# Transposing u by the DMA crossbar instead of on TensorE, with the loads of each stretch moved forward

## The chip, the cores and the metric

The kernel runs on one core of one Trainium2 chip. The metric is device time of one execution in microseconds (us). Times of one kernel mostly agree within 0.3%. Engines are named as in the profile: PE is TensorE's matmul stream, PEld its weight loads, DVE is VectorE, ACT is ScalarE, POOL is GpSimd, SP is SyncE, and SPq is SP's own queue, which issues DMAs one after the other. L followed by a number is a line of that kernel's file, so line numbers differ from kernel to kernel. A DMA's landing is the moment when its data are reported as in place; the granted clock is the share of PE's full clock that it was given.

## The reference, cut to what matters

Eight batches of 576 rows and 512 columns go through a retention layer (attention with a decay mask), then a mixer: a low-rank product over the sequence gives h, u = x + h, and a two-layer network runs on u.

```python
def _moe_ref(x, U, V, w_ch1, w_ch2):      # x: retention output, (8, 576, 512)
    xt = x.transpose(0, 2, 1)
    h = xt @ U @ V                         # rank 32, over the sequence
    u = x + h.transpose(0, 2, 1)
    ch = np.maximum(u @ w_ch1, 0.0) @ w_ch2   # 512 -> 2048 -> 512
    return (u + ch).astype(np.float32)
```

The first layer contracts over the 512 columns of u. TensorE contracts over partitions, so u, which is produced with rows on partitions, has to be transposed first. That transpose is what the change is about.

## The kernel before

Two batches form a pair of 1152 rows, which is nine chunks of 128 rows. An even batch takes four chunks into its network, an odd batch five. The work is merged into stretches: in the stretch of batch b the "main" list is the network of batch b (first layer Y1, then second layer Y2), and two "fill" lists are spread between its items: the attention and mixer of batch b+1, and "aux", the loads and preparations (cast, scaling, transposes of q and k by the crossbar) for later batches. A lead of 0.93 means that a fill's last item lies near 93% of the main list's matmul cost.

```python
LEAD = 0.93
def merge(main, *fills):
    total = sum(c for c, _ in main)
    ...
        queues.append([((k + 0.5) / n * LEAD * total, fn) for k, fn in enumerate(fill)])
    ...
# the mixer of one batch: MA (low rank), then per group of two chunks MH (h and u) and MT (transpose u)
outs = [(0, 1), (2, 3)] if par == 0 else [(4, 5), (6, 7), (8,)]
...
    def MT(grp):
        n, l0 = len(grp), grp[0] - base
        pu = ps_sc.tile([P, 2, NCC, P], BF16, tag="psc", name="pu")     # PSUM
        for s in range(n):
            for cc in range(NCC):                                       # NCC = 4
                nc.tensor.transpose(pu[:, s, cc, :],
                    st["u", par][:, l0 + s, cc * P:(cc + 1) * P], ident)
        nc.scalar.activation(out=st["uT", par][...], in_=pu[:, 0:n, :, :], func=AF.Copy)
...
    # first layer, for each of 16 blocks f of 128 columns
    for t0, n in segs:                     # [(0, 512)] even, [(0, 320), (320, 320)] odd
        for cc in range(NCC):
            nc.tensor.matmul(ps[:, 0:n], w1_sb[:, cc, f * P:(f + 1) * P],
                             st["uT", par][:, cc, t0:t0 + n], ...)
...
# aux, for chunk g: load(g) issues three DMAs on SP; prep(g - 2) casts, scales and issues
# one crossbar transpose of q and k, 128x1024, also on SP
for b in range(2, B):
    merge(y1_items(par) + y2_items(pr, par), fill, aux)
```

## Time and profile before

| | before |
|---|---|
| time, median | 366.6 us |
| PE busy from 98.5 to 289 us | 190.5 of 190.5 us |
| PE transposes of u | 144, in 20 groups |
| ACT evictions of uT | 20 |
| crossbar transposes on SP | 27, all of q and k, 128x1024 |

The table of busy time by stretch, kernel before. The columns are the window, its length, then busy time and instruction count of PE, PEld, DVE, ACT and POOL, then the granted clock of PE, the mean DMA share and GB/s.

```profile
98.50:134.50 36.00, 36.00 (x235) 17.27 (x233) 14.21 (x19) 6.35 (x10) 8.82 (x12) 1.00 0.84 189
134.50:169.40 34.90, 34.90 (x273) 17.26 (x271) 14.82 (x19) 16.69 (x28) 6.42 (x8) 1.00 0.60 134
169.40:211.40 42.00, 42.00 (x363) 25.20 (x361) 16.97 (x22) 20.74 (x44) 8.13 (x10) 1.00 0.76 157
```

PE is busy for the whole of each window. What leaves PE here should shorten the kernel; what leaves ACT should not.

The chain of waits in order of time, kernel before, at the end of batch 2's stretch (start, us, what):

```profile
161.63 0.43 PE ph L370 x2
162.06 0.45 PE pu L383 x8
162.50 1.73 PE ps_y L436 x8
164.23 0.22 PE ph L370
164.45 0.45 PE pu L383 x8
164.89 1.73 PE ps_y L436 x8
166.62 0.22 PE pu L383 x4
166.84 2.59 PE ps_y L436 x12
169.43 2.17 PE ps_y L415 x16
```

Eight transposes of u (pu) take 0.45 us, 56 ns each; eight 512-column matmuls take 1.73 us, 216 ns each. The last line is the first layer of batch 3, which starts with no gap.

The view of one tile, qkT, kernel before: the crossbar transposes that already exist (minimum, median and maximum of the time that SP's queue takes to issue one, in ns), and the time from issue to landing of all of them.

```profile
L201 SPq DMA_TRANSPOSE qkT<-qk x27: 1232/1253/4160, 65.2 to 284.3; - x27
DMA to landing us min/median/max: 3.0/3.2/6.5
```

Both maxima belong to the first transpose, at 65.2 us.

### The profile page before, as it was taken

What the parts mean: (1) busy time and instruction counts of PE and PEld (TensorE: products, weight loads), DVE (VectorE), ACT (ScalarE), POOL (GpSimd) and SP (SyncE); (2) the same over time, 40 slices, a digit from 0 to 9 for tenths busy, and PEclk for the clock granted to TensorE, in tenths of its full rate; (3) what the DMA queues carried; (4) which work ended last, traced back from release to release, by engine and by line L of the source; (5) the groups of instructions that cost most, each with busy time, mean ns of one, the idle gap of its engine ahead of it and who ended that gap; (6) DMA issues with size and microseconds to landing.
All of it is one profiled execution on the core that took longest, in us unless ns stands there. A gap on an engine that the chain in (4) does not pass through costs nothing.

```text
span 366.2 us, 6281 instructions
## 1 busy us (share of the span) xinstructions
PE 327.5 (89%) x2600; PEld 181.7 (50%) x2600; DVE 130.0 (36%) x180; ACT 162.3 (44%) x300; POOL 78.5 (21%) x114
## 2 busy tenths in 40 slices
PE   1466758899999999999999999999999999999990
PEld 0343334357644445545764545457754454567540
DVE  2354223442335414453343434443344144400110
ACT  4341446578710226425771266137732463258200
POOL 7166172220022240024102220122013100010010
PEclk9999978999999999999999999999999999999996
DMA  9999999997686982597567786786564300110010
GB/s 162 220 181 198 217 216 199 213 202 132 121 171 182 203 202 62 111 208 192 119 120 166 178 145 116 172 160 130 116 145 94 108 0 3 57 59 0 30 77 37
DMA packets 149820, 49.65 MB, mean 136 GB/s; under 512 B 143264, under 2 KB 147488, under 8 KB 149792
## 3 DMA queue, kind: packets, MB, share of 16 engines
q1 hardware_dynamic: 141024, 35.40, 51.9%
q0 software_dynamic: 8768, 13.86, 15.3%
q8 instruction: 20, 0.33, 0.4%
q14 instruction: 8, 0.07, 0.1%
HBM read 37.14 MB, written 9.44 MB: 127 GB/s over the span
## 4 chain that ended last, share of the span: by engine, by line
PE 50%; issue 28%; SPq 8%; POOL 5%; DMA 3%; ACT 2%; DVE 2%; POOLq 0%
PE ps_y L436 21%; PE ps_y L415 20%; SPq L174 8%; POOL vt L193 3%; PE psc L228 2%; PE po L267 2%; POOL out_dram L445 2%; DMA stage_t<-in_v_dram 1%; PE pu L383 1%; DMA stage_t<-in_q_dram 1%; DVE ret L238 1%; PE pss L293 1%; PE ph L370 1%; ACT qkT L214 1%; ACT y L420 1%
## 5 line engine op out<-in xcount | busy, mean ns | idle before, releaser
L415 PE MATMUL ps_y<-uT,w_sb 128*128 128x320 bf16 (+1 forms) x768 | 138.1, 330 | 3.5 <-ACT y L420 2.4
L436 PE MATMUL ps_y<-w_sb,y 128*128 128x512 bf16 x576 | 132.0, 379 | 0.0
L420 ACT ACTIVATE y<-ps_y 128x320 bf16<-128x320 f32 (+1 forms) x192 | 93.4, 490 | 53.6 <-PE ps_y L415 43.1
L415 PEld LDWEIGHTS <-w_sb 128*128 128x128 bf16 x768 | 72.4, 99 | 47.1 <-issue 5.9
L436 PEld LDWEIGHTS <-y 128*128 128x128 bf16 x576 | 54.0, 98 | 61.9 <-issue 2.5
L445 POOL DMA_DIRECT2D out_dram<-o_sb x36 | 20.3, 564 | 231.3 <-DVE o_sb L442 160.6
L238 DVE TENSOR_TENSOR ret<-psc,tri 128x1024 bf16<-128x1024 f32 x32 | 39.2, 1225 | 71.7 <-PE psc L228 71.7
L442 DVE TENSOR_TENSOR o_sb<-ps_y,u 128x512 f32<-128x512 f32 x36 | 24.8, 690 | 67.2 <-PE ps_y L436 67.1
L193 POOL TENSOR_TENSOR vt<-stage_t,vscale 128x512 bf16<-128x512 f32 x36 | 37.7, 1056 | 47.2 <-DMA stage_t<-in_v_dram 23.8
L387 ACT ACTIVATE uT<-pu 128x1024 bf16<-128x1024 bf16 (+1 forms) x20 | 18.8, 939 | 46.2 <-PE pu L383 46.2
L278 DVE TENSOR_TENSOR xt<-po,qscale 128x512 bf16<-128x512 f32 x36 | 24.9, 691 | 40.2 <-PE po L267 36.4
L373 DVE TENSOR_TENSOR u<-ph,xt 128x1024 bf16<-128x1024 f32 (+1 forms) x20 | 22.4, 1118 | 32.0 <-PE ph L370 32.0
L186 ACT ACTIVATE qk<-stage_t 128x512 bf16<-128x512 f32 x36 | 22.3, 623 | 10.4 <-DMA stage_t<-in_q_dram 10.4
L301 ACT ACTIVATE s_sb<-pss 128x512 bf16<-128x512 f32 x32 | 19.1, 596 | 17.0 <-PE pss L293 16.0
L351 ACT ACTIVATE a_sb<-pa 128x512 bf16<-128x512 f32 x8 | 4.8, 597 | 44.2 <-PE pa L346 44.2
L210 PE MATMUL pst<-ident,qk 128*128 128x128 bf16 x72 | 8.4, 288 | 15.1 <-ACT qk L186 15.1
L184 DVE CAST qk<-stage_t 128x512 bf16<-128x512 f32 x36 | 16.0, 444 | 10.3 <-DMA stage_t<-in_k_dram 10.3
L267 PE MATMUL po<-vt,ret 128*128 128x64 bf16 x288 | 15.6, 201 | 3.6 <-DVE ret L238 2.8
L267 PEld LDWEIGHTS <-ret 128*128 128x128 bf16 x288 | 13.7, 103 | 10.0 <-DVE ret L238 4.0
L228 PE MATMUL psc<-qkT 64*128 64x128 bf16 x288 | 15.6, 233 | 2.7 <-DVE ret L238 1.3
L228 PEld LDWEIGHTS <-qkT 64*128 64x128 bf16 x288 | 8.9, 100 | 15.5 <-issue 10.9
L210 PEld LDWEIGHTS <-qk 128*128 128x128 bf16 x72 | 6.8, 132 | 17.7 <-ACT qk L186 16.5
(47 smaller groups left out, 125.0 us busy)
## 6 DMA issues: line engine op xcount, KB each, us to landing
out_dram<-o_sb POOLq DMA_DIRECT2D x36, 256.0 KB, 2.8
stage_t<-in_k_dram SPq DMA_DIRECT2D x32, 256.0 KB, 4.1
stage_t<-in_q_dram SPq DMA_DIRECT2D x32, 256.0 KB, 4.7
stage_t<-in_v_dram SPq DMA_DIRECT2D x32, 256.0 KB, 5.1
w_sb<-in_moe_w_ch_dram POOLq DMA_DIRECT2D x16, 128.0 KB, 6.8
w_sb<-in_moe_w_ch_dram POOLq DMA_DIRECT2D x8, 256.0 KB, 9.4
stage_t<-in_k_dram SPq DMA_DIRECT2D x8, 128.0 KB, 3.4
stage_t<-in_q_dram SPq DMA_DIRECT2D x8, 128.0 KB, 3.6
```

What stands on the lines that cost most here:

```text
L174: nc.sync.dma_start(out=c["f"][rows, j, :, :], in_=dram[b, :, t0:t0 + n, :].rearrange("h s d -> s h d"),)
L193: nc.gpsimd.tensor_tensor(out=c["v"], in0=c["f"][:, 2, :, :], in1=vscale[:, i, :, None].to_broadcast([P, H, D]), op=ALU.mult,)
L228: nc.tensor.matmul(psc[:, hl, hp, :], qkT[r, NHP + hp, :], qkT[r, hp, :], start=True, stop=True,)
L238: nc.vector.tensor_tensor(out=ret.rearrange("p (hp hl) i -> p hl hp i", hl=2), in0=c["psc"], in1=m[:, None, None, :].to_broadcast([P, 2, N ...
L267: nc.tensor.matmul(c["po"][:, hl, hp * D:(hp + 1) * D], c["ret"][:, h, :], c["v"][:, h, :], start=(first and hp == 0), stop=True, skip_gro ...
L278: nc.vector.tensor_tensor(out=xt[:, i, :].rearrange("p (hp hl d) -> p hl hp d", hl=2, d=D), in0=c["po"][:, :, 0:NHP * D].rearrange("p hl ( ...
L373: nc.vector.tensor_tensor(out=st["u", par][:, i0 - base:i0 - base + n, :], in0=ph[:, 0:n, :], in1=st["x", pr][:, i0:i0 + n, :], op=ALU.add,)
L415: nc.tensor.matmul(ps[:, 0:n], w1_sb[:, cc, f * P:(f + 1) * P], st["uT", par][:, cc, t0:t0 + n], start=(cc == 0), stop=(cc == NCC - 1),)
L420: nc.scalar.activation(out=st["y1", par][:, f, t0:t0 + n], in_=ps[:, 0:n], func=AF.Relu)
L436: nc.tensor.matmul(ps, st["y1", par][:, f, c * P:(c + 1) * P], w2_sb[:, f, :], start=(f == 0), stop=(f == NF - 1),)
L442: nc.vector.tensor_tensor(out=o_sb, in0=ps, in1=st["u", par][:, c, :], op=ALU.add)
L445: nc.gpsimd.dma_start(out=out_flat[r0:r0 + P, :], in_=o_sb)
```

## The change

From batch 2 on, u is no longer transposed on PE and evicted by ACT. Each chunk, 128x512, goes through the DMA crossbar from SBUF to SBUF, issued on SP right after u of its group exists. The aux list now ends near 0.7 of the stretch, so that the loads pause when these transposes need SP and the DMA engines. The other fill ends near 0.9.

```diff
-LEAD = 0.93
-def merge(main, *fills):
+def merge(main, *fills, leads=(0.9, 0.7)):
...
-        queues.append([((k + 0.5) / n * LEAD * total, fn) for k, fn in enumerate(fill)])
+        queues.append([((k + 0.5) / n * lead * total, fn) for k, fn in enumerate(fill)])
...
         def MT(grp):
             n, l0 = len(grp), grp[0] - base
+            if pr > 0:
+                for s in range(n):
+                    nc.sync.dma_start_transpose(
+                        out=st["uT", par][:, :, (l0 + s) * P:(l0 + s + 1) * P],
+                        in_=st["u", par][:, l0 + s, :],
+                    )
+                return
...
                 if m < len(outs):
                     MH(outs[m])
-                if m > 0:
+                if pr > 0:
+                    if m < len(outs):
+                        MT(outs[m])
+                elif m > 0:
                     MT(outs[m - 1])
```

More of the change, by code (lines that the diff above doesn't have):

```diff
@@ L13 @@
 ALU = mybir.AluOpType
-LEAD = 0.93
-def merge(main, *fills):
+def merge(main, *fills, leads=(0.9, 0.7)):
     total = sum(c for c, _ in main)
     queues = []
-    for fill in fills:
+    for fill, lead in zip(fills, leads):
         n = len(fill)
-        queues.append([((k + 0.5) / n * LEAD * total, fn) for k, fn in enumerate(fill)])
+        queues.append([((k + 0.5) / n * lead * total, fn) for k, fn in enumerate(fill)])
     done = 0.0
```

## The prediction

> **What bounds the kernel now.** From about 85 us on, TensorE. The table of busy time by stretch gives PE 36.00 of 36.00 us in 98.5-134.5, 34.90 of 34.90 in 134.5-169.4, 42.00 of 42.00 in 169.4-211.4, and so on to about 349 us, at granted clock 1.00; DVE and ACT are about 40-50% busy. Before 85 us the start-up bounds: DMA share 9 tenths, and a chain of waits over load issues and ACT/DVE hand-offs. The change hardly touches that part.
>
> **Removed.** Batches 2 to 7 have 27 row chunks of u, four 128x128 transposes each: 108 of the 144 PE transposes. In the chain, eight take 0.45 us of PE (56 ns each), so 108 x 56 ns = 6.0 us, all where PE is never idle: all on the critical path. Also 15 ACT evictions of uT (1.02 us, 0.60 for the half tile), about 14 us off the path: worth nearly nothing.
>
> **Added.** 27 crossbar transposes of 128x512 on the SP queue. The 27 existing ones of 128x1024 take SP 1.23 us to issue and land after 3.1-3.2 us in the steady part (6.5 at worst, while loads saturated the queues at 65 us). I estimate half the issue, 0.65 us, plus the same tail of 1.9 us: 2.5 us alone, 3.2 us for two in a row. The Trainium skill ("DMA: Bandwidth & Descriptors", Issuing engines are not separate DMA queues) says all DMAs share the same 16 engines and interleave; the 6.5 us agrees. Hence the change's second half: loads end at about 0.66 of a stretch's matmul work and the u transposes come after.
>
> **Is the new latency hidden?** In the changed instruction order, a batch's last h matmul is followed by 28 second-layer matmuls (28 x 216 ns = 6.05 us) where an even batch comes next, 24 (5.2 us) where an odd one does, 44 at the first boundary. Even: DVE add 1.23, hand-offs 0.2, transposes 3.2: about 4.7 us. Odd: one chunk, 0.69 + 0.2 + 2.5 = 3.4 us. Both fit with over 1 us to spare: no PE stall, or a few tenths at one or two boundaries.
>
> **Moved.** A chunk's load comes every 5.9 us rather than 7.8. Queue 1 took 51.9% of the span for 36 chunks and 27 transposes, about 5 us each, so the DMA share rises to 0.85-0.95 in the load part. Casts come two loads (11 us) after issue, against landings of 4-7 us, so ACT and DVE should not stall. In the stretch after start-up (48-85 us) casts come earlier, but after the loads land; its remaining PE transposes sit closer (12 in a row): perhaps 0.4 us lost.
>
> **Prediction.** 366.6 - 6.0 + 0.2 to 0.4 = 360.8 us (-1.6%), range 359.3 to 363.3. Faster by over 2%: 0.10; within 2%: 0.86; slower: 0.04.
>
> **What would show it.** pu transposes fall from 144 to 36, uT evictions from 20 to 5; each stretch from 98 us on shortens by 0.9 (even batch's transposes gone) or 1.1 us (odd); u transposes land within 2.2-3.5 us; first-layer matmuls wait under 1 us in total for uT.
>
> **What would make it wrong.** The 128x512 transposes landing in 4 us or more (or traffic still in the queues): a stall at each of six boundaries, where 1 us each eats the gain. SP stuck on a late cast ahead of them. ACT starved of casts by compressed loads, with PE stalls in first-layer phases. Or the first stretch shifting by over 1 us.

## The result, and the profile after

The changed kernel takes 363.57 us (four runs, 363.13 to 363.83) against 366.6 us: ratio 0.991, 95% interval 0.989 to 0.993. A ratio here and below is the mean time of one kernel's fast runs over that of the other's fast runs of the same rounds, so it is not quite the ratio of the medians. Executions over 1.5% slower than the fastest of the same kernel are left out of the means. The gain is 3.0 us where 5.8 were forecast, and the time lies 0.3 us outside the range. The single profiled executions differ by 4.2 us (spans 366.2 and 362.0), but there the first layer of batch 0 happens to start 1.1 us earlier; I therefore compare stretches, not spans.

The same windows, kernel after:

```profile
98.50:134.50 36.00, 35.59 (x209) 16.41 (x213) 14.30 (x19) 3.68 (x7) 8.41 (x13) 1.00 0.92 190
134.50:169.40 34.90, 33.76 (x255) 16.77 (x259) 14.81 (x19) 14.57 (x27) 7.42 (x10) 1.00 0.77 163
169.40:211.40 42.00, 41.75 (x343) 24.03 (x345) 17.73 (x22) 18.85 (x43) 7.75 (x11) 1.00 0.88 172
```

In the middle window PE now shows 1.1 us without work: 0.7 us are one wait, explained below, and 0.3 us are two gaps of 0.15 to 0.16 us with 7 matmuls shown in place of 8, which I take to be missing records. The DMA share has risen by 0.08 to 0.17.

SP's timeline, kernel after, around the end of batch 2's stretch (start, us, what, count):

```profile
155.99 2.44 SPq L199 DMA_TRANSPOSE qkT<-qk  x1
158.58 6.64 SPq L380 DMA_TRANSPOSE uT<-u  x5
165.32 0.74 SPq L172 DMA_DIRECT2D stage_t<-in_k_dram  x1
```

PE's timeline, the same time:

```profile
161.01 0.38 PE L368 MATMUL ph<-a_sb,V 128*128 128x512 bf16 x1
161.23 5.34 PE L444 MATMUL ps_y<-w_sb,y 128*128 128x512 bf16 x24
166.41 0.71 PE L423 MATMUL ps_y<-uT,w_sb 128*128 128x320 bf16 x4
167.84 1.79 PE L423 MATMUL ps_y<-uT,w_sb 128*128 128x320 bf16 x12 [0.72 <-DMA uT<-u]
```

And the chain of waits there (short pieces left out):

```profile
161.43 0.70 DVE u L371
162.13 0.46 SPq L380
162.63 1.27 SPq L380
164.00 3.71 DMA uT<-u
167.84 1.79 PE ps_y L423 x12
```

The last h matmul is followed by 24 second-layer matmuls, as I had read from the instruction order. The add that makes the last chunk of u ends at 162.1. But SP is still issuing: the chain goes over the end of one transpose (0.46) and a whole one (1.27) before the fifth counts as under way at 164.0, and its data are there after 167.7. The first segment of the first layer (four matmuls) needs three chunks only and starts at 166.4; the second segment waits.

The tile view of uT, kernel after, gives the cost that I had estimated as half of 1.23 us:

```profile
L380 SPq DMA_TRANSPOSE uT<-u x27: 1188/1239/1982, 121.5 to 316.5; - x27
DMA to landing us min/median/max: 2.4/2.8/4.4
```

A transpose of half the width takes SP the same 1.24 us. The list of waits names the price:

```profile
PE ps_y L423 <- DMA uT<-u: 2.0, 3, 0.9
```

This is 2.0 us in total, three times, 0.9 at most: at the three boundaries where an odd batch (five chunks) begins, none at the three where an even batch (four chunks) begins.

The clearest account is the length of a stretch, from the first Y1 matmul of a batch to that of the next, read from PE's timeline in each profile (us):

| kernel | batch 2 | batch 3 | batch 4 | batch 5 | batch 6 |
|---|---|---|---|---|---|
| before | 34.93 | 41.99 | 34.93 | 42.00 | 34.93 |
| after | 33.82 | 42.22 | 33.81 | 42.14 | 33.82 |
| e2: no transposes of u at all | 33.81 | 41.34 | 33.82 | 41.09 | 33.82 |
| e4: one issue for a pair of chunks | 33.81 | 41.23 | 33.81 | 41.11 | 33.81 |
| e6: fill ends at 0.80 | 34.88 | 41.10 | 34.88 | 41.10 | 34.83 |
| e7: loads do not pause | 33.81 | 51.52 | 33.81 | 49.71 | 33.81 |

Even stretches gain the full 1.1 us (the 20 transposes of an odd batch, 20 x 56 ns). Odd ones should gain 0.9 and lose 0.1 to 0.2 instead, because each begins with the wait. (Against e2 each loses 0.16 to 0.17 us more than its wait in the list, which is counted only from the modelled end of the last matmul.)

### The profile page after: what moved, and what is told of

The parts are those of the page before. It is cut to its first block, busy times and chain, and to the rows that moved or that the text cites. A ratio compares the mean times of both kernels' runs of the same rounds, so it can differ in the third digit from the quotient of the medians.

```text
span 362.0 us, 6084 instructions
## 1 busy us (share of the span) xinstructions
PE 318.3 (88%) x2462; PEld 174.9 (48%) x2492; DVE 132.3 (37%) x180; ACT 147.7 (41%) x285; POOL 77.8 (21%) x114
## 4 chain that ended last, share of the span: by engine, by line
PE 47%; issue 26%; SPq 10%; DMA 6%; POOL 4%; ACT 3%; DVE 2%; POOLq 0%; ACTq 0%
PE ps_y L423 21%; PE ps_y L444 18%; SPq L172 8%; DMA stage_t<-in_v_dram 3%; PE psc L226 2%; DMA uT<-u 2%; POOL out_dram L453 2%; PE po L265 2%; SPq L380 2%; POOL vt L191 1%; PE pss L291 1%; DMA stage_t<-in_q_dram 1%; PE ph L368 1%; DVE ret L236 1%; ACT qkT L212 1%
## 5 line engine op out<-in xcount | busy, mean ns | idle before, releaser
L444 PE MATMUL ps_y<-w_sb,y 128*128 128x512 bf16 x560 | 129.0, 379 | 0.9 <-issue 0.3
L182 DVE CAST qk<-stage_t 128x512 bf16<-128x512 f32 x36 | 17.6, 488 | 9.1 <-DMA stage_t<-in_k_dram 9.1
L208 PE MATMUL pst<-ident,qk 128*128 128x128 bf16 x72 | 7.6, 270 | 14.1 <-ACT qk L184 14.1
L291 PE MATMUL pss<-vt,qk 128*128 128x128 bf16 (+1 forms) x128 | 13.8, 236 | 0.4 <-ACT s_sb L299 0.3
L208 PEld LDWEIGHTS <-qk 128*128 128x128 bf16 x72 | 6.0, 122 | 16.3 <-ACT qk L184 15.1
```

The lines of the kernel that those rows point to most:

```text
L444: nc.tensor.matmul(ps, st["y1", par][:, f, c * P:(c + 1) * P], w2_sb[:, f, :], start=(f == 0), stop=(f == NF - 1),)
```

## The experiments

Theory A: SP needs about 1.24 us to issue a crossbar transpose whatever its width, so the five of an odd batch leave SP too late. Its rivals are that the leads cost the 3 us (B), that a PE transpose was worth less than 56 ns (C), that the transposes are late because the DMA engines are full (D), and that issue time does go with width (F). The first four runs shared one chip and its runs of before (median 366.88 us), the last four another set (367.13 us).

### e1: the leads alone

```diff
-            if pr > 0:
+            if False:          # PE transposes everywhere; leads stay (0.9, 0.7)
```

> Only the second half of the change: the two lead factors, with all 144 PE transposes kept. Theory A (the missing 3 us is lost where an odd batch's first layer waits for the crossbar transposes, because each one takes SP about 1.24 us to issue whatever its width): the leads alone cost little, ratio 0.998 to 1.003 to before. Rival B (the compressed loads or the re-packed first stretch cost the 3 us): this run is about 3 us slower than before, ratio near 1.008.

Measured: 367.48 us, ratio 1.0018, interval 0.9995 to 1.0041. Rival B falls: the leads cost about 0.6 us, and not clearly more than nothing. In the trace the re-packed PE transposes of batch 1 wait 1.11 us for an eviction (kernel before: 0.25 us), as e8 takes up.

### e2: no transpose at all

```diff
             if pr > 0:
-                for s in range(n):
-                    nc.sync.dma_start_transpose(...)
                 return
...
+                if pr == 0:                # keep the uT of batches 0 and 1
                     st["uT", 0] = uT_pool.tile(...)     # and the same for st["uT", 1]
```

> Wrong result on purpose: for batches 2 to 7 u is not transposed at all, the first layer reads the old uT of batches 0 and 1; leads as in the change. It measures what taking 108 PE transposes away is worth when nothing takes their place. Theory A: the full 6.0 us, so about 360.6 us, ratio 0.983 to 0.985. Rival C (a PE transpose is worth less than 56 ns in these stretches): about 363.5 us, ratio 0.991, like the change itself.

Measured: 361.44 us, ratio 0.985, interval 0.983 to 0.987 (the result is wrong). That is 5.4 us below before, and 6.0 below e1, which has the same leads. Rival C falls. The change misses this floor by 0.0064 of 366.9 us, 2.3 us, and the table above finds them: 0.88 + 1.05 us in the odd stretches of batches 3 and 5, and 0.52 us in batch 7, whose first layer takes 17.90 us to its first Y2 matmul after the change and 17.38 without transposes.

### e3 and e4: the same bytes in 27 issues or in 15

A pair of chunks can be transposed by one instruction of 128x1024 only if its blocks land one behind the other: with the old layout of uT the output has four dimensions, and that does not build ("Output must optimize to 2/3D shape"). Both runs therefore lay uT out by chunk, and e3 is the control.

```diff
-    uT_pool.tile([P, NCC, 5 * P], ...)          # and 4 * P for an even batch
+    uT_pool.tile([P, 5, NCC, P], ...)
-    segs = ... [(0, 320), (320, 320)]
+    segs = ... [(0, 384), (384, 256)]
...   # PE's transposes of batches 0 and 1 and the first layer read and write this layout
 # e4 only, e3 keeps one issue for each chunk:
-    for s in range(n):
-        nc.sync.dma_start_transpose(out=st["uT", par][:, l0 + s, :, :], in_=st["u", par][:, l0 + s, :])
+    nc.sync.dma_start_transpose(
+        out=st["uT", par][:, l0:l0 + n, :, :].rearrange("p s c t -> p (s c) t"),
+        in_=st["u", par][:, l0:l0 + n, :].rearrange("p s d -> p (s d)"))
```

> Control for the next run: the change with uT laid out chunk by chunk, so that first-layer segments of an odd batch are 384 and 256 columns in place of 320 and 320; still one crossbar transpose per chunk (27 of them). Theory A and rival D (traffic): as the change, 363.0 to 364.0 us, ratio about 0.991; five issues in a row of 1.24 us each at an odd boundary, first layer waits 0.7 to 1.0 us there.

> As the control, but one crossbar transpose for each pair of chunks (128x1024), so 15 issues instead of 27, the same bytes. Theory A: an issue still takes about 1.24 us, so an odd boundary has 3 issues in place of 5, the last starts as soon as its DVE add is done and the wait vanishes: 361.0 us, ratio about 0.985. Rival D (the transposes are late because the DMA engines are full of load traffic, not because of the issue): landing times stay at 3 to 4.4 us and the waits remain, ratio about 0.991.

Measured: e3 363.74 us, ratio 0.9907 (0.989 to 0.993), as the change. e4 361.15 us, ratio 0.9839 (0.982 to 0.986). The tile view of uT in e4, then PE's timeline at the same boundary:

```profile
L379 SPq DMA_TRANSPOSE uT<-u x15: 1219/1232/1355, 122.3 to 313.0; - x15
DMA to landing us min/median/max: 2.4/3.1/4.0
```

```profile
161.81 0.38 PE L368 MATMUL ph<-a_sb,V 128*128 128x512 bf16 x1
162.03 5.34 PE L443 MATMUL ps_y<-w_sb,y 128*128 128x512 bf16 x24
167.21 2.34 PE L422 MATMUL ps_y<-uT,w_sb 128*128 128x384 bf16 x16
```

The add that makes the last chunk of u, and the issue of its transpose, in e4:

```profile
162.23 0.69 DVE L371 TENSOR_TENSOR u<-ph,xt 128x512 bf16<-128x512 f32 x1 [0.55 <-PE ph L368]
163.09 1.22 SPq L379 DMA_TRANSPOSE uT<-u  x1
```

Twice the width, the same 1.23 us of issue, and a median landing no faster (3.1 us against 2.8). Yet no first-layer matmul waits for uT, and the stretches equal those of e2 within 0.11 us. What is gone is the queue on SP: before batches 3, 5 and 7 the last transpose is issued 0.17, 0.16 and 0.14 us after its add, where after the change it was 1.87, 2.83 and 2.39 us. Rival D falls as an explanation of all three waits: the bytes are the same and the DMA engines were no emptier (share 0.99 in 158.5-165.5 us, against 0.86 in 158.5-165.3 us after the change), and the last transpose lands 2.5, 3.1 and 2.4 us after its issue, against 3.7, 2.9 and 2.8. Before batch 3 the landing did have a part, 1.2 us; I have not traced why. But without the 1.7 us of queue alone its data would have been there at 166.0 (an estimate from the chain), before PE came to need them at about 167. (Issuing half of the transposes from ACT would not be a simple way out: the Trainium skill, "DMA: Bandwidth & Descriptors", DMA Transpose (X-bar), says that two streams of transposes in flight together can corrupt each other's results, so one must wait for the other. No run here shows that.)

### e5: the same bytes in 54 issues

```diff
+                    for h2 in range(2):        # two transposes of 128x256 for each chunk
                         nc.sync.dma_start_transpose(
-                            out=st["uT", par][:, :, (l0 + s) * P:(l0 + s + 1) * P],
-                            in_=st["u", par][:, l0 + s, :])
+                            out=st["uT", par][:, 2 * h2:2 * h2 + 2, (l0 + s) * P:(l0 + s + 1) * P],
+                            in_=st["u", par][:, l0 + s, h2 * 256:(h2 + 1) * 256])
```

> The change with each crossbar transpose cut in two halves of 128x256: 54 issues, the same bytes, the same leads. Theory A (issue time is per transpose, not per byte): each still takes SP about 1.2 us, so an odd boundary has ten issues, 12 us, and an even one eight; the last lands some 5 us after the first layer could start at the three odd boundaries and about 3 us after at two even ones: 376 to 386 us. Rival F (issue time goes with the width, as I had estimated: 0.3 us each): as the change, about 363.6 us.

Measured: 397.35 us, ratio 1.082. The tile view of uT in e5:

```profile
L381 SPq DMA_TRANSPOSE uT<-u x54: 1167/1244/2178, 121.0 to 347.5; - x54
DMA to landing us min/median/max: 2.3/2.4/3.6
```

A quarter of e4's width costs nearly the same to issue: 1.24 us in the median (the shortest took 1.17, 1.19 and 1.23 us at 256, 512 and 1024 columns). Rival F, which was my prediction's own estimate, falls. The loss is larger than theory A forecast (376 to 386 us). PE's timeline shows waits of about 21 us in all at the boundaries from batch 3 on. The rest is a lowered clock: five times it falls to half, for 30.7 us in all, in which PE is busy for 23.3; at half clock that costs 11.7 us (an estimate). With the 19 us of waits beyond the change's own this makes 31 of the 32 us by which the two profiled runs differ. The busy time around one of these falls (columns as before; the clock is the third number from the end):

```profile
302.33:305.74 3.41, 0.84 (x4) 0.13 (x2) 0.69 (x1) 0.00 (x0) 0.54 (x1) 1.00 0.48 126
305.74:312.57 6.83, 5.97 (x17) 2.11 (x18) 0.00 (x0) 2.39 (x4) 0.00 (x0) 0.50 0.02 5
```

It follows a wait of 2.5 us.

### e6: more slack in place of fewer issues

```diff
-            merge(y1_items(par) + y2_items(pr, par), fill, aux)
+            merge(y1_items(par) + y2_items(pr, par), fill, aux, leads=(0.8, 0.7))
```

> The change with the attention and mixer work of batches 3 to 7 ending at 0.80 of the stretch rather than 0.90 (fill lead 0.8 in the merges from batch 2 on), still 27 issues of 128x512. Theory A: the last h matmul comes about 2.5 us earlier before an odd boundary, more than the 1 us that is missing, so the waits for uT vanish: 361.0 to 361.8 us, ratio about 0.985. If PE loses the 3 us elsewhere, no change from 0.991.

Measured: 364.15 us, ratio 0.992 (0.990 to 0.994). This expectation missed. The waits for uT are indeed gone, and the odd stretches reach 41.10 us. But each even stretch became 1.07 us longer: the attention and mixer of the next odd batch, packed into 0.8 of the stretch, now make PE wait for DVE. PE's timeline in e6, at two points of batch 2's stretch:

```profile
146.55 0.41 PE L265 MATMUL po<-vt,ret 128*128 128x64 bf16 x8 [0.24 <-DVE ret L236]
159.68 0.38 PE L368 MATMUL ph<-a_sb,V 128*128 128x512 bf16 x1 [0.49 <-DVE u L371]
```

These two waits account for 0.73 of the 1.07 us and recur, at nearly these sizes, in batches 4 and 6; I have not traced the rest. The missing slack can be found by starting earlier, but in this schedule it is paid for elsewhere.

### e7: the transposes without the pause of the loads

```diff
-def merge(main, *fills, leads=(0.9, 0.7)):
+def merge(main, *fills, leads=(0.93, 0.93)):
```

> The crossbar transposes with both leads as before (0.93): what the pause of the loads is worth. Theory A: the u transposes now queue on SP behind loads and q/k transposes (about 3.4 us of issue per chunk) and start later, so each boundary from batch 3 on loses 1 to 3 us: 365 to 369 us, no better than the kernel before. If the pause is worth nothing, 363.5 us or less.

Measured: 383.38 us, ratio 1.045, far worse than forecast. SP's timeline in e7, end of batch 2's stretch:

```profile
159.55 5.24 SPq L380 DMA_TRANSPOSE uT<-u  x4
164.90 0.53 SPq L172 DMA_DIRECT2D stage_t<-in_k_dram  x1
165.47 0.70 SPq L172 DMA_DIRECT2D stage_t<-in_q_dram  x1
166.22 0.99 SPq L172 DMA_DIRECT2D stage_t<-in_v_dram  x1
167.31 2.14 SPq L380 DMA_TRANSPOSE uT<-u  x1
```

A chunk's load stands in SP's queue between the fourth and the fifth transpose, so the fifth starts 2.5 us after the fourth has been issued (167.31 against 164.79), with the DMA engines full of that load; its issue then takes 2.14 us and it lands 5.1 us after it began. So here the load in front costs twice, on SP and in the landing. PE's timeline, and then the busy time by stretch in e7:

```profile
166.52 0.71 PE L423 MATMUL ps_y<-uT,w_sb 128*128 128x320 bf16 x4
172.52 3.27 PE L423 MATMUL ps_y<-uT,w_sb 128*128 128x320 bf16 x12 [5.30 <-DMA uT<-u]
```

```profile
166.00:172.50 6.50, 1.22 (x8) 0.50 (x6) 0.69 (x1) 0.44 (x1) 2.68 (x3) 0.97 1.23 242
172.50:176.00 3.50, 3.48 (x20) 1.82 (x20) 0.00 (x0) 1.05 (x3) 0.00 (x0) 0.56 1.23 231
176.00:180.00 4.00, 4.00 (x44) 3.00 (x39) 2.25 (x3) 2.96 (x8) 1.04 (x1) 1.00 0.04 6
```

After 5.3 us of waiting PE runs for 3.5 us at a granted clock of 0.56. The Trainium skill ("TensorE: Matmul & The Clock Gate", Part 1) says that PE's clock falls to half after an idle window of about 3.4 us and returns after as long a busy one. This stretch agrees; e5 does not quite: there the clock fell five times after 3.41 us in which PE had been busy for 0.43 to 1.34 us. Nor does length alone decide: a wait of 3.33 us in e7 (before 218.0) left the clock at 1.00, as did those of 0.7 and 0.9 us in the changed kernel. So a boundary wait costs its own length while it is short, and can cost more from 2.5 us on. In e7 PE waits five times for uT, 16.4 us in all, also before two even batches; 14.4 us of this are beyond the change's own, and two spells at half clock (6.8 us, PE busy for 6.3) cost some 3.1 us more by the same estimate as in e5: 17.5 of the 17.7 us between the two profiled runs. This is what made e5 and e7 worse than I expected. Without the pause of the loads the crossbar transposes would have been a loss of 16 us.

### e8: an attempt to beat both

```diff
 # e4, and in the first merge alone, where batch 1 still transposes on PE:
-    merge(y1_items(0), attn_items(0, 1, T=True) + mixer_items(0, 1), aux_items(NI, NI + 5))
+    merge(y1_items(0), attn_items(0, 1, T=True) + mixer_items(0, 1), aux_items(NI, NI + 5),
+          leads=(0.93, 0.93))
```

> Attempt to beat both: one transpose per pair of chunks as in e4, and the old leads (0.93, 0.93) in the first merge alone, where batch 1 still transposes on PE and the new leads put 12 PE transposes in a row with a gap of 1.11 us. I expect 0.3 to 0.8 us less than e4's ratio 0.984, so 0.982 to 0.983.

Measured: 360.77 us, ratio 0.9828, interval 0.981 to 0.985. The wait of 1.11 us in the first merge is back to 0.25, and the result is correct. It is the fastest kernel, 6.4 us under before and below the change. Its advantage over e4 (ratio 0.9839) is inside the intervals, so the gain of the first merge's leads is not shown; the gain of the merged issue is.

## Why the prediction was wrong

1. **"108 x 56 ns = 6.0 us, all on the critical path": right.** e2 measured it, 5.4 us with the leads' cost inside and 6.0 without.
2. **ACT evictions "worth nearly nothing": consistent.** ACT was busy at most about half of each stretch, and e2, which drops both transposes and evictions, gains just what the PE transposes account for.
3. **"I estimate half the issue, 0.65 us": wrong, and the root of the step that failed.** The trace measured 1.24 us at 128x512, and e4 and e5 nearly the same at 128x1024 and 128x256. I had one width to read from and took issue time to scale with it. The sum "2.5 us alone" came out right by luck: the quickest transposes landed after 2.4 to 2.5 us, but as 1.24 of issue and some 1.2 of tail, not 0.65 and 1.9.
4. **"Odd: one chunk, 0.69 + 0.2 + 2.5 = 3.4 us": this is the step that failed.** It took the last chunk alone, as if SP were free when it arrived; with 0.65 us an issue it nearly would have been (an estimate from the times of the adds). With 1.24 us each, five issues fill 6.5 to 6.6 us of SP, the last one queues behind the fourth for 1.9 to 2.8 us, a term that the sum did not have, and before batch 3 the span from last h matmul to data was about 6.5 us (161.2 to 167.7) against the 5.2 us of slack that I had read correctly. There the landing took 3.7 us in place of 2.5 as well. Even batches, with four issues and 6 us of slack, showed no wait, as predicted.
5. **"First-layer matmuls wait under 1 us in total for uT": wrong.** It was 2.0 us by the list of waits, and 2.45 us by the lengths of the stretches (0.88 + 1.05 + 0.52 against e2). This is most of the missing gain of 2.8 us, and e4 removes it without touching a byte.
6. **"Perhaps 0.4 us lost" in the first stretch: not contradicted.** e1 measured 0.6 us for all the leads, with an interval that includes zero.
7. **"ACT and DVE should not stall" on the compressed loads: right as far as PE shows.** e2 keeps the compressed loads, and its stretches are shorter than those of before by just what the transposes took, but for 0.25 us in batch 3 that e1 shows as well (42.24 against 41.99 us).
8. Among the things that could make it wrong I had named a stall at the boundaries, but from slow landing. The median landing of 2.8 us lay within the 2.2 to 3.5 that I had given, the longest (4.4) outside it; of the three last chunks, which decide, only the one before batch 3 landed later than 3.5. What I had not named was the queue of issues.

## What to carry to other kernels

Count the instructions on a DMA queue, not only their bytes: here a crossbar transpose cost about 1.2 us of its issuer's time at each of the three widths tried, so join neighbouring transposes into one, even if a tile has to be laid out anew. When a result is handed from one stage to the next by DMA, add up the whole queue of issues before the last one, including those just ahead of it, and compare that with the slack. An experiment that leaves the disputed operation out altogether gives the floor, and lengths of stretches against that floor show where the rest went.

## What the Trainium skill lacked or had wrong

- "DMA: Bandwidth & Descriptors", DMA Transpose (X-bar): I found there no issue time of a crossbar transpose on trn2 (elsewhere the skill has one duration for a 128x128 transpose, without saying what it covers, and cycles of unnamed earlier generations). The runs show 1.17 to 1.25 us on SP, minimum to median, for 128x256, 128x512 and 128x1024 alike, landing 2.3 to 3.2 us after issue (minimum to median) in SBUF-to-SBUF use.
- The same page, Issuing engines are not separate DMA queues, calls the sequencer's time to start a DMA usually small against the DMA itself. For these transposes it was 1.24 us of 2.4 to 2.8 us (minimum to median), and the number of issues alone was worth 2.6 us (e4 against e3, by the medians, with the same bytes).
- The same page, Rules for kernel authors, advises to coalesce small transfers and names those under 64 KB; it lacks that joining transposes of 128 KB (128x512 in bf16) still pays where SP's queue is what is waited for: 54, 27 and 15 issues of the same bytes took 397.35, 363.57 and 361.15 us (the last with uT laid out by chunk, which alone changed nothing: 363.74 us).
- "TensorE: Matmul & The Clock Gate", Part 1, was borne out in part: clock 0.56 for 3.5 us after a wait of 5.3 us (e7), and 1.00 after waits of 0.7 and 0.9 us. But it names an idle window of about 3.4 us, and in e5 the clock fell to half after 3.41 us with PE busy for 0.43 to 1.34 us of them, once after a wait of only 2.5 us.
